# One visit to TensorE's quarters for two pairs of heads, tails and k^T v in rotating banks, and the mean as two products

## The chip, the cores and the metric

The kernel runs on one core of one Trainium2 chip. The metric is device microseconds (us) of one execution. The median of three runs before the change is 900.35 us (900.15 to 900.92).

## The reference

The first part is a linear attention over 8 sequences, 8 heads, 576 rows and 64 columns per head; its result, read as 4608 rows of 512, goes through a gated MLP with 2048 hidden columns. All is float32.

```python
kv = np.einsum('bhsd,bhse->bhde', k, v)
out = np.einsum('bhsd,bhde->bhse', q, kv)
rms = np.sqrt(np.mean(out * out, axis=-1, keepdims=True) + 1e-06)
x = out / rms * g_norm            # then (B,H,S,D) -> (B*S, H*D)
h = x @ w_in
sp = np.maximum(h, 0.0) + np.log1p(np.exp(-np.abs(h)))
g = h * erf(sp)
return g @ w_out
```

## The kernel before

**Groups, batches, pairs.** The MLP works on nine groups of 512 rows, numbered T = 0 to 8. Groups 0 to 7 are the first 512 rows of a sequence each; group 8 collects the eight tails of 64 rows, kept in `x_last`. Groups 0 and 1 run in a plain stage (the loop at L976); from group 2 on the loop at L1143 runs one batch of four hidden units per step. Batch m is b = m mod 4 of group T = m div 4, so batches 8 to 11 are group 2. While group T runs in the MLP, the attention of group T+1 is computed in its batches, one pair of heads (p = 0 to 3) to a batch; that of group 2 runs in the plain stage's group 1.

**A batch on TensorE.** Each batch has eight "products" (L588): four hidden ones (units i = 0 to 3 of this batch: x times w_in) and four results (j = 0 to 3: gated values of the batch before times w_out). A product splits float32 into three float32r parts: eight matmuls of 512 columns into a bank `n_ps`, then four into a bank `m_ps`. ScalarE copies the hidden `n_ps` out (L1192), VectorE adds `m_ps` (L574); results are added into `e` by VectorE alone (L569 or L1129, and L574).

**Banks.** PSUM has eight banks. Six, two named `h` and four `o0` to `o3`, rotate: `pair_of_banks` (L578) takes the first two of the list and puts them at its end, so a product gets its banks back three products later. The other two form the tile `at` of the attention.

**A pair of heads in the attention (L379, `apart` for groups 3 to 7).** Pairs are also numbered i = 4T + p. Its steps in this order:
- `loads`: the DMA starts for k, v and q of the pair after next go onto a list, `to_fetch`. q comes in eight small transfers (L153), laid out so that VectorE's 32x32 transpose (`turn`, L332) gives q^T.
- `visit` (L404): TensorE is used as four quarters of 64x64. Four products of 256 columns give o = q kv (L411); two of 64 columns give the tail's rows (L419); 18 give k^T v of the next pair (L425), all into `at`. A float32 product is two instructions on TensorE. `kv_products` (L338) alternates between the diagonal quarters and the others, so each pair of heads leaves two half sums. Then ScalarE squares o.
- `halve` (L443): VectorE splits the square into two float32r parts. `keep_tail` (L432): one copy of the tail, then `kv_kept` (L354): two copies and one addition that join the half sums of k^T v into `bd_kv`.
- `turn` of the next pair.
- `mean` (L450): four matmuls of 256 columns with the matrix `mean_w`, into the unused half of `at`; ScalarE then does ln, exp and a square.
- `norm` (L481): three VectorE instructions, of which the first (L483) is the last reader of the mean. `split` makes the three parts of x for the next group.

**Where the steps stand.** The loop calls `pieces(place)` with places 0 to 8: place i+1 follows hidden product i, place 5+j follows result j. The steps stand at places (0, 2, 3, 5, 6, 8): loads at 0, visit with halve and keep_tail at 2, that is between hidden products 1 and 2, turn at 3, mean at 5, norm at 6, split at 8. In a group's last batch they are (0, 2, 3, 4, 5, 5, 6). Groups T+1 = 8 use `attention` with other places, no visit, and a mean of two matmuls of 512 columns.

**DMA.** SP issues nearly all transfers in order. At each of the eight fetch places (after product 0, 1, ... 7) it issues the weights that `FETCH` (L1140) names, then two entries of `to_fetch`. The first results of a group's first batch finish the group before, so each is followed by a store that waits for VectorE. w_out has seven buffers; the fourth load for the next batch is the last weight load of the batch.

Of the kernel before, what the change touches and what calls it, by code (L numbers as in the profile page):

```python
# [39 lines left out]
FP32 = mybir.dt.float32  # L40
FP32R = mybir.dt.float32r
I32 = mybir.dt.int32
U32 = mybir.dt.uint32
AF = mybir.ActivationFunctionType
ALU = mybir.AluOpType
PSUM = bass.MemoryType.PSUM

EPS = 1e-6
# [7 lines left out]
FIRST = 2  # L56
# [12 lines left out]
def kernel(  # L69
# [10 lines left out]
    nc = tc.nc  # L80
    P = 128
    B, H, S, D = q.shape
    DM, DF = moe_w_in.shape[0], moe_w_in.shape[1] // 2
    J = 4
    G = J * P
    R = S - G
    NP = H // 2
# [6 lines left out]
    kvp = ctx.enter_context(tc.tile_pool(name="kvp", bufs=2))  # L94
    attp = ctx.enter_context(tc.tile_pool(name="attp", bufs=1))
# [8 lines left out]
    early = early_room.enter_context(tc.tile_pool(name="early", bufs=2))  # L104
# [6 lines left out]
    def exp_ln_table():  # L111
        nc.scalar.preload_act_table_set("natural_log_exp_and_others")

    def softplus_table():
        nc.scalar.preload_act_table_set("softplus")  # L115
# [11 lines left out]
    def load_pair(i, later=False):  # L127
        T, p = divmod(i, NP)
        if T >= B:
            return  # L130
        pool = early if i in (2, 3) else kvp
        for name, got, src in (("k", k_sb, k), ("v", v_sb, v)):
            side = nc.scalar if (i, name) == (0, "v") else nc.sync
            t = got[T, p] = pool.tile([P, CH, D], FP32, name=f"{name}_sb", tag=name)
            start = partial(
                side.dma_start,
                out=t.rearrange("r c d -> r (c d)"),
                in_=src[T, 2 * p : 2 * p + 2].rearrange("h (r c) d -> (h r) (c d)", c=CH),
            )
            if later:  # L140
                to_fetch.append(start)
            else:
                start()
        if T > 0:
            load_q(i)
            return
        t = pool.tile([P, G if pool is early else S], FP32, name="q_sb", tag="q")
        t = q_sb[T, p] = t[:, 0:G].rearrange("p (j h d) -> p j h d", j=J, h=2)
        nc.sync.dma_start(
            out=t, in_=q[T, 2 * p : 2 * p + 2, 0:G, :].rearrange("h (p j) d -> p j h d", j=J)  # L150
        )

    def load_q(i):  # L153


        T, p = divmod(i, NP)
        t = q_sb[T, p] = kvp.tile([P, S], FP32, name="q_sb", tag="q")
        for n in range(P // SQ):
            h, w = divmod(n, D // SQ)
            to = t[n * SQ : n * SQ + SQ].rearrange("a (j b) -> a j b", b=SQ)  # L160
            for head, js in ((1 - h, slice(0, G // 2 // SQ)), (h, slice(G // 2 // SQ, S // SQ))):
                src = q[T, 2 * p + head, :, w * SQ : w * SQ + SQ]
                to_fetch.append(
                    partial(
                        nc.sync.dma_start,
                        out=to[:, js],
                        in_=src.rearrange("(j a) b -> a j b", a=SQ)[:, js],
                    )
                )
# [153 lines left out]
    def halves_of(t):  # L323
        return t.rearrange("p (a t) -> p a t", a=2)

    def kv_of(T, p):
        return bd_kv[:, (T * NP + p) % 2, :]

    def qt_tile(name):
        return attp.tile([P, S], FP32, name=name, tag="qT")  # L330

    def turn(T, p):  # L332

        if T < B:
            qT = ready[T, p] = qt_tile("qT")
            nc.vector.transpose(out=qT, in_=q_sb.pop((T, p)))

    def kv_products(T, p, at, first=0):  # L338


        ks, vs = (x.pop((T, p)) for x in (k_sb, v_sb))
        for c in range(CH):
            for i, rows in enumerate(rows_of):
                half = (i + c + first) % 2
                yield partial(
                    nc.tensor.matmul,
                    at[rows_of[half], 1 if half == i else 0, kv_cols],
                    lhsT=ks[rows, c],
                    rhs=vs[rows, c],
                    start=(c < 2),  # L350
                    stop=(c >= CH - 2),
                )

    def kv_kept(T, p, at):  # L354


        kv = kv_of(T, p).rearrange("p (a e) -> p a e", a=2)
        other = attp.tile([P, 2, D], FP32, name="kv_other", tag="kv_other")
        for i in range(2):
            nc.vector.tensor_copy(out=other[rows_of[i]], in_=at[rows_of[1 - i], ::-1, kv_cols])  # L360
        nc.vector.tensor_tensor(out=kv, in0=at[:, :, kv_cols], in1=other, op=ALU.add)

    def at_tile():
        return at_pool(1).tile([P, 2, G], FP32, name="at_ps", tag="at")

    def prepare(T, p):

        at = at_tile()
        for product_ in kv_products(T, p, at):
            product_()  # L370
        kept.append(partial(kv_kept, T, p, at))

# [6 lines left out]
    def attention(T, p, in_parts=False):  # L379
# [2 lines left out]

        halves = T > 1 or (T == 1 and p > 0)
        quad = T < B
        apart = FIRST < T < B
        then = divmod(T * NP + p + 1, NP)

        def two(t):
            return halves_of(t) if quad else t
# [6 lines left out]
            return ps_now[0].tile([P, G], FP32, name=name, tag="at")  # L396

        def square_tile(name):

            if apart:  # L400
                return attp.tile([P, G], FP32, name=name, tag="sq_lo")
            return qt_tile(name)[:, 0:G]

        def visit():  # L404


            qT = ready.pop((T, p))
            at = st["at"] = at_tile()
            x = halves_of(qT[:, 0:G])
            for a, i in ((0, 0), (0, 1), (1, 0), (1, 1)):  # L410
                nc.tensor.matmul(  # L411
                    at[rows_of[i if a else 1 - i], a, 0 : 2 * P],
                    lhsT=bd[rows_of[i], a * D : (a + 1) * D],
                    rhs=x[rows_of[i], a],
                    start=True,
                    stop=True,
                )
            for s in rows_of:
                nc.tensor.matmul(  # L419
                    at[s, 1, 2 * P : 2 * P + R], lhsT=bd[s, D : 2 * D], rhs=qT[s, G:S], start=True, stop=True  # L420
                )
            st["o"] = at[:, :, 0 : 2 * P]
            if then[0] < B:
                for product_ in kv_products(*then, at, first=1):
                    product_()  # L425
            if apart:
                st["sq"] = x_new.tile([P, G], FP32, name="sq", tag="x")
            else:
                st["sq"] = qT[:, 0:G]
            nc.scalar.activation(two(st["sq"]), st["o"], AF.Square)  # L430

        def keep_tail():  # L432
            nc.vector.tensor_copy(
                out=x_last[:, p, T * R : T * R + R], in_=st["at"][:, 1, 2 * P : 2 * P + R]
            )
            if then[0] < B:
                kv_kept(*then, st["at"])

        def square():
            st["o"], st["sq"] = x_last[:, p, :], square_tile("sq")  # L440
# [73 lines left out]
            split_lower()  # L514

        def loads():
            load_pair(T * NP + p + 2, later=True)

        after = (split_upper, split_lower) if in_parts else (split,)
        if T == B:  # L520
# [1 line left out]

        first_ = (partial(prepare, T, p),) if (T, p) == (1, 0) else ()
        then_ = partial(turn, *then)
        if apart:
            pieces = ((loads,), (visit, halve, keep_tail), (then_,))
            return (*(partial(chain, *group) for group in pieces), mean, norm, *after)
        pieces = (first_, (visit, loads), (halve, keep_tail) if halves else (keep_tail,))
        return (*(partial(chain, *group) for group in pieces), mean, partial(chain, norm, then_), *after)


    def upper(x, high):

        nc.scalar.activation(high, x, AF.Copy, scale=1.0 + 2.0**-13)  # L534
# [14 lines left out]
    def lower(x, high, low, both):  # L549
        lower_only(x, high, low)  # L550
        both_only(high, low, both)
# [26 lines left out]
    def pair_of_banks(*names, turns=True):  # L578
        pair = tuple(
            pool.tile([P, G], FP32, name=name, tag=tag)  # L580
            for name, (pool, tag) in zip(names, banks[:2])
        )
        if turns:
            banks.extend(banks[:2])
            del banks[:2]
        return pair

    def product(weights, moving, turns=True, cuts=()):  # L588

# [104 lines left out]
    def first_group(p):  # L694
# [3 lines left out]

        def kv():
            st["kv"] = at_tile() if p == 0 else ps_now[0].tile([P, 2, G], FP32, name="kv_ps", tag="at")  # L700
            for product_ in kv_products(0, p, st["kv"]):
                product_()

        def kv_out():
# [438 lines left out]
    for m in range(first_batch, batches + 1):  # L1143
# [1 line left out]
        todo = []  # L1145
        last_ = b == NB - 1 and T + 1 < NG
        if T + 1 < NG:
            todo = list(attention(T + 1, b, in_parts=last_))
            if b == 0:
                side = late_r if T % 2 == FIRST % 2 else late  # L1150
                forms = side.tile([P, 3, KC, G], FP32R, name=f"x_forms{(T + 1) % 2}")
                x_forms[T + 1] = [forms[:, i] for i in range(3)]
# [133 lines left out]
```

## Time and profile before

| | |
|---|---|
| median of three runs | 900.35 us |
| profiled execution | 900.88 us, span of its instructions 899.1 us |
| granted TensorE clock | 0.999 |
| TensorE busy | 891.6 us (99%) |
| VectorE busy | 765.5 us (85%) |
| ScalarE busy | 594.8 us (66%) |
| moved by DMA | 259.89 MB, 289 GB/s |

The span runs from the first to the last instruction; the execution's own time also has 1.8 us around it. Busy shares are means over stages: batches 8 to 26 are the stage of the change, batches 27 to 31 and group 8 have other work. Matmuls overlap in the trace, so their cost is read from starts. A wait that ends in "issue" has nothing in the profile to blame.

### The profile page before, as it was taken

What the parts mean: (1) busy time and instruction counts of PE and PEld (TensorE: products, weight loads), DVE (VectorE), ACT (ScalarE), POOL (GpSimd) and SP (SyncE); (2) the same over time, 40 slices, a digit from 0 to 9 for tenths busy, and PEclk for the clock granted to TensorE, in tenths of its full rate; (3) what the DMA queues carried; (4) which work ended last, traced back from release to release, by engine and by line L of the source; (5) the groups of instructions that cost most, each with busy time, mean ns of one, the idle gap of its engine ahead of it and who ended that gap; (6) DMA issues with size and microseconds to landing.
All of it is one profiled execution on the core that took longest, in us unless ns stands there. A gap on an engine that the chain in (4) does not pass through costs nothing.

```text
span 899.1 us, 13468 instructions
## 1 busy us (share of the span) xinstructions
PE 891.6 (99%) x4962; PEld 670.6 (75%) x4962; DVE 765.5 (85%) x1105; ACT 594.8 (66%) x789; POOL 4.7 (1%) x14
## 2 busy tenths in 40 slices
PE   8999999999999999999999999999999999999998
PEld 4444456666788888888888888888888888888887
DVE  5899978899799888888888888888888888886667
ACT  5976677777766666666766666666666666665552
POOL 2000000000000000000000000000000000000000
PEclk9999999999999999999999999999999999999999
DMA  9977318899699987998899979998897787778871
GB/s 285 295 221 232 110 73 320 306 340 351 236 383 356 354 299 263 381 310 302 267 362 337 318 258 327 361 305 293 292 348 274 267 320 296 287 286 315 320 264 49
DMA packets 136929, 259.89 MB, mean 289 GB/s; under 512 B 78816, under 2 KB 87264, under 8 KB 136864
## 3 DMA queue, kind: packets, MB, share of 16 engines
q1 hardware_dynamic: 136128, 258.09, 81.3%
q8 instruction: 39, 0.64, 0.3%
q10 hardware_dynamic: 544, 0.82, 0.2%
q14 instruction: 26, 0.21, 0.1%
q0 software_dynamic: 192, 0.13, 0.1%
HBM read 224.40 MB, written 34.60 MB: 288 GB/s over the span
## 4 chain that ended last, share of the span: by engine, by line
PE 97%; ACT 2%; DVE 1%; issue 0%; DVEq 0%; ACTq 0%
PE n_ps L599 50%; PE m_ps L599 25%; PE o_ps L655 9%; PE h_ps L1021 5%; PE at_ps L411 2%; PE at_ps L425 2%; PE n_ps L918 1%; PE at_ps L463 1%; PE at_ps L464 1%; PE warm_ps L802 1%; PE o_ps L918 0%; ACT w_m L260 0%; PE o_ps L722 0%; DVE w_in_sb L281 0%; DVE w_e L276 0%
## 5 line engine op out<-in xcount | busy, mean ns | idle before, releaser
L599 PE MATMUL n_ps<-w_out_parts,g_forms 128*128 128x512 f32 (+1 forms) x936 | 230.7, 389 | 0.0
L599 PE MATMUL n_ps<-x_forms,w_in_parts 128*128 128x512 f32 x896 | 224.2, 392 | 0.0
L599 PEld LDWEIGHTS n_ps<-w_out_parts,g_forms 128*128 128x128 f32 x936 | 173.8, 188 | 35.3
L599 PEld LDWEIGHTS n_ps<-x_forms,w_in_parts 128*128 128x128 f32 x896 | 166.6, 188 | 35.3
L574 DVE TENSOR_TENSOR h<-m_ps,h 128x512 f32<-128x512 f32 x116 | 78.1, 687 | 60.0 <-PE m_ps L599 56.0
L599 PE MATMUL m_ps<-w_out_parts,g_forms 128*128 128x512 f32 x464 | 124.0, 389 | 0.0
L599 PE MATMUL m_ps<-x_forms,w_in_parts 128*128 128x512 f32 x448 | 119.9, 389 | 0.0
L1192 ACT ACTIVATE h<-n_ps 128x512 f32<-128x512 f32 x112 | 66.1, 593 | 74.9 <-PE n_ps L599 74.7
L1197 ACT ACTIVATE s<-h 128x512 f32<-128x512 f32 x112 | 68.3, 629 | 70.1 <-DVE h L574 70.1
L599 PEld LDWEIGHTS m_ps<-w_out_parts,g_forms 128*128 128x128 f32 x464 | 87.1, 188 | 18.5
L599 PEld LDWEIGHTS m_ps<-x_forms,w_in_parts 128*128 128x128 f32 x448 | 84.1, 188 | 17.9
L574 DVE TENSOR_TENSOR e<-m_ps,e 128x512 f32<-128x512 f32 x116 | 80.1, 692 | 15.2 <-PE m_ps L599 5.4
L655 PE MATMUL o_ps<-w_out_sb,h_sb 128*128 128x512 f32 x192 | 86.8, 595 | 0.0
L540 DVE SCALAR_TENSOR_TENSOR g_forms<-g_forms 128x1024 fp32r<-128x1024 f32 x58 | 71.1, 1225 | 2.0
L537 DVE TENSOR_TENSOR g_forms<-h,g_forms 128x1024 fp32r<-128x1024 f32 x58 | 70.5, 1216 | 1.2 <-ACT g_forms L534 1.1
L534 ACT ACTIVATE g_forms<-h 128x1024 fp32r<-128x1024 f32 x58 | 58.4, 1049 | 15.5 <-PE m_ps L599 11.1
L569 DVE SCALAR_TENSOR_TENSOR e<-n_ps,e 128x512 f32<-128x512 f32 (+1 forms) x89 | 60.3, 678 | 6.9 <-PE n_ps L599 6.9
L1246 DVE TENSOR_TENSOR h<-h,s 128x1024 f32<-128x1024 f32 x56 | 65.9, 1217 | 0.0
L655 PEld LDWEIGHTS o_ps<-w_out_sb,h_sb 128*128 128x128 f32 x192 | 35.5, 190 | 38.3 <-issue 36.9
L1021 PE MATMUL h_ps<-xT,w_in_sb 128*128 128x512 f32 x128 | 57.9, 596 | 1.3 <-DVE w_in_sb L281 1.2
L115 ACT ACT_TABLE_LOAD x43 | 55.2, 1283 | 0.8
L1220 ACT ACTIVATE s<-s 128x1024 f32<-128x1024 f32 x50 | 50.6, 1054 | 0.3
(148 smaller groups left out, 1018.7 us busy)
## 6 DMA issues: line engine op xcount, KB each, us to landing
w_out_parts<-w_out SPq DMA_DIRECT2D x116, 768.0 KB, 7.1
w_in_parts<-w_in SPq DMA_DIRECT2D x112, 768.0 KB, 6.9
w_in<-w_new SPq DMA_DIRECT2D x16, 768.0 KB, 4.5
k_sb<-in_k_dram SPq DMA_DIRECT2D x32, 288.0 KB, 5.9
v_sb<-in_v_dram SPq DMA_DIRECT2D x31, 288.0 KB, 5.7
w_raw<-in_moe_w_in_dram SPq DMA_DIRECT2D x16, 512.0 KB, 5.7
w_raw<-in_moe_w_out_dram SPq DMA_DIRECT2D x8, 1024.0 KB, 4.8
out_dram<-e SPq DMA_DIRECT2D x32, 256.0 KB, 3.7
```

What stands on the lines that cost most here:

```text
L115: nc.scalar.preload_act_table_set("softplus")
L534: nc.scalar.activation(high, x, AF.Copy, scale=1.0 + 2.0**-13)
L537: nc.vector.tensor_tensor(out=low, in0=x, in1=high.bitcast(FP32), op=ALU.subtract)
L540: nc.vector.scalar_tensor_tensor(out=both, in0=low.bitcast(FP32), scalar=SHIFT, in1=high.bitcast(FP32), op0=ALU.mult, op1=ALU.add,)
L569: nc.vector.scalar_tensor_tensor(out=out_, in0=ps, scalar=scale, in1=out_, op0=ALU.mult, op1=ALU.add)
L574: nc.vector.tensor_tensor(out=out_, in0=ps, in1=out_, op=ALU.add)
L599: nc.tensor.matmul(ps[:, cols], lhsT=weights(form, k), rhs=moving(form, k)[:, cols], start=(form == forms[0] and k == 0), stop=(form == fo ...
L655: nc.tensor.matmul(o_ps[j], lhsT=g[:, j * P : j * P + P], rhs=one(w_out_sb, f), start=(f == 0), stop=last,)
L1021: nc.tensor.matmul(plain[i], lhsT=blocks_of(one(w_in_sb, i % FC))[:, c], rhs=xT[T][:, c, :], start=(c == 0), stop=(c == KC - 1),)
L1192: nc.scalar.activation(h[:, i], n_ps, AF.Copy, scale=SHIFT - 1.0)
L1197: nc.scalar.activation(s[:, i], h[:, i], AF.Softplus)
L1246: nc.vector.tensor_tensor(out=part(h, half), in0=part(h, half), in1=part(s, half), op=ALU.mult)
```

## The change

For groups 3 to 7 a function `paired` replaces `attention`. It takes the pairs of heads two by two; "first batch" and "second batch" below mean the batches with even and odd p.

- First batch: at place 0 the sixteen q transfers of the next two pairs go onto the list (for pair 12, the first of group 3, also the transpose of pair 13). At place 2 one visit for both pairs: eight products of 256 columns, which fill `at`, then four tail products and 36 for k^T v of the next two pairs. The tails and k^T v go to two banks from the rotation, diagonal quarters to one, the others to the second, issued two and two. Then the square and halves of the first pair, one copy for both tails, four copies and two additions for both k^T v (`two_kept`), and the k, v transfers of two later pairs. Nothing at place 3.
- Second batch: nothing at place 0; at place 2 the square of the second pair from the same `at`, and its halves; at place 3 two transposes.
- Both: the mean is two matmuls of 512 columns into one bank of the rotation (`next_bank`); norm and split as before, o read from `at`.
- The last visit in `attention` (group 2, pair 3) also makes k^T v of the second pair of group 3. k and v of pairs 13 to 15 are loaded earlier. q^T has two buffers (2304 bytes a partition more), `kv_other` is 512 bytes larger.

```diff
     def qt_tile(name):
-        return attp.tile([P, S], FP32, name=name, tag="qT")
+        return attp.tile([P, S], FP32, name=name, tag="qT", bufs=2)
...
-    def kv_products(T, p, at, first=0):
+    def kv_products(T, p, diagonal, beside, first=0):
...
-                yield partial(
+                yield half == i, partial(
                     nc.tensor.matmul,
-                    at[rows_of[half], 1 if half == i else 0, kv_cols],
+                    (diagonal if half == i else beside)[rows_of[half]],
...
+    def two_kept(diagonal, beside):
+        kv = bd_kv.rearrange("p n (a e) -> p n a e", a=2)
+        other = other_tile(2)
+        for i in range(2):
+            for a, ps in enumerate((diagonal, beside)):
+                nc.vector.tensor_copy(out=other[rows_of[i], :, a], in_=ps[rows_of[1 - i]])
+        for a, ps in enumerate((beside, diagonal)):
+            nc.vector.tensor_tensor(out=kv[:, :, a], in0=ps, in1=other[:, :, a], op=ALU.add)
...
+            if both:
+                for _, product_ in kv_products(then[0], 1, at[:, 1, more_cols], at[:, 0, more_cols]):
+                    product_()
...
         def loads():
-            load_pair(T * NP + p + 2, later=True)
+            i = T * NP + p + 2
+            if i == (FIRST + 1) * NP + 1:
+                load_q(i)
+                load_kv(i + 1)
+                load_kv(i + 2)
+                return
+            load_pair(i, later=True)
+            if i == (FIRST + 1) * NP:
+                load_kv(i + 1)
...
+    def paired(T, p, in_parts=False):
...
+        def visit():
+            at = twice["at"] = at_tile()
+            qs = [ready.pop((T, p + n)) for n in range(2)]
+            for n in range(2):
+                x, bd = halves_of(qs[n][:, 0:G]), kv_of(T, p + n)
+                for a, r in ((0, 0), (0, 1), (1, 0), (1, 1)):
+                    nc.tensor.matmul(
+                        at[rows_of[r if a else 1 - r], a, n * 2 * P : (n + 1) * 2 * P],
...
+            small = pair_of_banks("diag_ps", "off_ps")
...
+            for n in range(2 if more else 0):
+                for on, product_ in kv_products(
+                    *divmod(i + 2 + n, NP), kv_diag(n), kv_off(n), first=1
+                ):
+                    (diag if on else off).append(product_)
+            while diag or off:
+                for some in (diag, off):
+                    for product_ in some[:2]:
+                        product_()
+                    del some[:2]
...
+        def mean(table=True):
+            ms = st["ms"] = next_bank("ms_ps")
+            nc.tensor.matmul(ms, lhsT=mean_w, rhs=st.pop("hi"), start=True, stop=False)
+            nc.tensor.matmul(ms, lhsT=mean_w, rhs=st.pop("lo"), start=False, stop=True)
...
+        def q_loads():
+            if i == (FIRST + 1) * NP:
+                turn(T, 1)
+            for n in range(2):
+                load_q(i + 2 + n)
+
+        def kv_loads():
+            for n in range(2):
+                load_kv(i + 4 + n)
+
+        def turns():
+            for n in range(2):
+                turn(*divmod(i + 1 + n, NP))
+
+        if side == 0:
+            start = (q_loads, partial(chain, visit, square, halve, keep, kv_loads), chain)
+        else:
+            start = (chain, partial(chain, square, halve), turns)
+        return (*start, mean, norm, *after)
...
+    def next_bank(name):
+        pool, tag = banks[0]
+        banks.append(banks.pop(0))
+        return pool.tile([P, G], FP32, name=name, tag=tag)
...
-            todo = list(attention(T + 1, b, in_parts=last_))
+            todo = list((attention if T + 1 == B else paired)(T + 1, b, in_parts=last_))
```

## The prediction

> **What bounds the kernel now.** I read the chain that ended last first: it says which engine's work has to shrink.
>
> ```profile
> PE 97%; ACT 2%; DVE 1%; issue 0%; DVEq 0%; ACTq 0%
> ```
>
> TensorE carries 97% of it, so time is won only by making TensorE's stream shorter, and lost only where it is made to wait. Next I read TensorE's timeline over batch 10 (from 281.60; batches count from group 0, batch 8 starts at 234.13), in the middle of the stage that is changed: start in us, duration of the merged row, operation.
>
> ```profile
> 286.13 1.07 PE L599 MATMUL m_ps<-x_forms,w_in_parts 128*128 128x512 f32 x4
> 287.13 0.66 PE L411 MATMUL at_ps<-qT,bd_kv 64*64 64x256 f32 x8
> 287.61 0.22 PE L425 MATMUL at_ps<-v_sb,k_sb 64*64 64x64 f32 x2
> ...
> 288.30 2.12 PE L599 MATMUL n_ps<-x_forms,w_in_parts 128*128 128x512 f32 x8
> 290.26 1.08 PE L599 MATMUL m_ps<-x_forms,w_in_parts 128*128 128x512 f32 x4
> 291.18 1.98 PE L599 MATMUL n_ps<-x_forms,w_in_parts 128*128 128x512 f32 x8
> ...
> 293.90 1.98 PE L599 MATMUL n_ps<-w_out_parts,g_forms 128*128 128x512 f32 x8
> ...
> 296.62 0.28 PE L463 MATMUL at_ps<-sq_hi,mean_w 128*128 128x256 f32 x1
> ...
> 297.09 2.03 PE L599 MATMUL n_ps<-w_out_parts,g_forms 128*128 128x512 f32 x8
> ...
> 299.87 1.98 PE L599 MATMUL n_ps<-w_out_parts,g_forms 128*128 128x512 f32 x8
> ```
>
> Durations overlap, so I go by starts. An undisturbed product takes 2.72 us (291.18 to 293.90); its last four products, on m_ps, 0.91. The visit costs what lies between 286.13 and 291.18 beyond 0.91 and one product: 5.05 - 3.63 = **1.42**. The mean costs 299.87 - 296.62 - 2.72 = **0.53**. And 8 x 2.72 + 1.42 + 0.53 = 23.71, which is the distance between visits (287.13 to 310.84): TensorE waits for nothing here. The windows give 20.9 us of VectorE and 15.5 of ScalarE in such a batch: both have slack.
>
> **The visit, step by step.** 287.04 (286.13 + 0.91) to 287.13: 0.09 to enter. To 287.61: 0.48 for the eight instructions of q (a float32 product is two), two in each of four quarters. To 288.30: 0.69 for 40 instructions of 64 columns. How much of that is work shows in batch 27, whose visit has only the four tail instructions:
>
> ```profile
> 690.75 0.28 PE L419 MATMUL at_ps<-qT,bd_kv 64*64 64x64 f32 x4
> 690.96 2.12 PE L599 MATMUL n_ps<-x_forms,w_in_parts 128*128 128x512 f32 x8
> ```
>
> There it is 0.21 for two rounds; here 0.69 for ten (40 / 4). So a round takes 0.06 (0.058 by the unrounded starts) and 0.11 is exit. The product after the visit is 0.16 too long. Fixed are 0.09 + 0.11 + 0.16 = 0.36, plus 0.05 of q's first round, whose matmuls are the longest (L411 by tile: 376 to 428 ns).
>
> A visit for two pairs: q 0.48 + 0.43, then 4 tails and 36 k^T v products. With first=1 each pair has ten products for the off-diagonal quarters, eight for the diagonal ones, plus two tails: 20 and 20, issued two and two, so 20 full rounds, 1.16. Sum 0.09 + 0.91 + 1.16 + 0.11 + 0.16 = 2.43 against 2 x 1.42: **0.41 saved, ten times, 4.1 us**. The trace has no visit of this length: from below, nothing of 0.41 is saved if changing pair or bank in mid-visit costs an exit and entry again; from above 0.46, if the rounds also lose the 0.05 at q's second pair. I take 0.41, the row with the same instructions; visits of 4 and 40 small instructions differ by rounds alone.
>
> Two visits change length. That of the third group's last pair (at 215.16, in the plain stage) takes the k^T v of a second pair: 9 or 10 rounds, +0.55. The last one covers batches 26 and 27, which cost 1.42 and 0.95 now: 0.09 + 0.91 + 4 x 0.058 + 0.11 + 0.16 = 1.50, 0.46 better than counted. Net **-0.1**.
>
> **The mean as two products.** The trace has it: in batch 28, for the last group,
>
> ```profile
> 721.57 0.39 PE L463 MATMUL ms_ps<-sq_hi,mean_w 128*128 128x512 f32 x1
> ...
> 724.77 1.98 PE L599 MATMUL n_ps<-w_out_parts,g_forms 128*128 128x512 f32 x8
> ```
>
> 3.20 - 2.72 = 0.48 against 0.53. Saved 0.05, twenty times: **1.0 us**. The Trainium skill, "TensorE: Matmul & The Clock Gate", section "Back-to-back issue gap", speaks against a gain here: 262 cycles for 256 columns and 518 for 512 would make four products 1048 cycles and two 1036, an estimate of 0.005 us a mean and 0.1 in all. The rows of this trace decide for 1.0.
>
> TensorE's sum: 4.1 + 1.0 - 0.1 = **5.0 us**. The second qT tile and the wider kv_other move later tiles in SBUF; no row here depends on a tile's place (L574 takes 0.69 on both of its tiles), so that costs nothing.
>
> **The other engines.** VectorE does the same copies for two pairs at once: one tail copy (0.22 for 64 columns), four of 0.29, two additions of 0.29, about 2.0 against 1.1. In the first batch they replace a transpose (0.77) and stand after both halves of the square, ahead of the third addition to h. Counted from the batch's start: the third product starts at 5.44 + 0.09 + 0.91 + 1.16 + 0.11 = 7.71, the square 0.15 later as now (288.45 after 288.30), then 0.6 of square, 1.15 of halves, 2.0 of copies: 11.7. Result 0, which takes the copies' two banks next, starts at 7.71 + 2.88 + 2.72 = 13.3, and VectorE was idle for 1.34 us before the fourth addition to h, which takes up the delay. The second batch has two transposes (1.54), no copies, and lasts 21.76 + 0.48 = 22.24, as batches 28 to 30 do without a stall; VectorE has 20.9 - 1.1 + 0.8 = 20.6 in it. The Trainium skill, "TensorEngine Tiling (Array Packing)", section "PSUM Bottleneck", warns that copying out of PSUM may become the bound once the array is packed; by that rule the second batch would go at VectorE's pace, still 1.6 us below TensorE's, and the sum would stay.
>
> Banks: six rotate in pairs; a visit now takes two of them and each mean one. The visit's pair held result 3 of the batch before, whose additions end 2.6 us into the batch; it is written at 6.4. The third product gets the first one's pair back after two products instead of three: its m_ps part starts at 9.7, and both additions to h that free these banks end at 7.5 (289.13 in batch 10). The tight place is the mean's bank: it is m_ps of result 3, two products later. VectorE frees it here (batch 13; result 3 starts at 373.73, its m_ps part at 375.54):
>
> ```profile
> 371.21 0.69 DVE L574 TENSOR_TENSOR e<-m_ps,e 128x512 f32<-128x512 f32 x1 [0.23 <-PE m_ps L599]
> 371.82 2.35 DVE L1246 TENSOR_TENSOR h<-h,s 128x1024 f32<-128x1024 f32 x2
> 374.09 0.68 DVE L483 SCALAR_TENSOR_TENSOR u<-at_ps,u 128x512 f32<-128x512 f32 x1
> ```
>
> The end, 374.77, leaves 0.77 us (in a group's last batch, where the mean comes earlier, it is result 2's bank, with 2.1). Bounds: nothing lost, or whatever VectorE is later than 0.77. I take nothing for ordinary batches, since VectorE waits for TensorE just ahead (the 0.23).
>
> **Loads.** SP gets 16 q pieces in a first batch, two at each of its eight places, where k, v and eight pieces filled the first five; four k, v go to the second batch's first two places. The k, v of pairs 13 to 15 go out in the plain stage, where DMA is busy 0.68 of the time (216 to 240). In the second batch the results start at 10.88 us, not 12.30, and need the last w_out. Where stores go out (first batch of a group) SP holds it back until VectorE has finished result 2:
>
> ```profile
> 353.99 0.34 SPq L670 DMA_DIRECT2D out_dram<-e  x1
> 354.38 0.93 SPq L844 DMA_DIRECT2D w_out_parts<-w_out  x2
> ```
>
> The second of these (354.90) landed 6.8 us later, 8.96 into its batch: 1.9 us remain of 3.3. Behind it come the last two q pieces, then the store; k, issued there now, took 7.2 and landed at 10.3, and the second transpose would start at 10.2. In batch 9 the same load was issued at 260.59 and took 9.0: 11.70 into the batch. There results wait up to 0.8; q, landing about 12.5, holds VectorE two more, which pass through the fourth addition, softplus, erf and rms to the mean's bank. The batch before it is 1.0 longer, which gives DMA that much. I charge **0.8 us** once (bounds 0 and 2.5), and nothing for the four others (bounds 0 and 1 each).
>
> **Forecast.** The profiled execution took 900.88 (span 899.1); 5.0 - 0.8 = 4.2 off makes 896.7. It lay 0.53 above the median of the runs, so the median goes from 900.35 to **896.1**.
>
> **Rivals.**
> *Clean:* no load is late: 900.35 - 5.0 = 895.3. For it: waits of TensorE for DMA are absent from the waits. Against: batch 9.
> *The visit saves nothing:* a drain inside the visit at each change of pair or bank. Only the mean remains: 900.35 - 1.0 + 0.1 + 0.8, about 900.2; half saved, 898.2. Against it: within a visit rows follow at 0.06 through all changes of operand.
> *Partly late:* loads cost 0.7 in each of the other four second batches after a store: 896.1 + 2.8 = 898.9.
> *Slower:* the same place, further. The last w_out and q of the second batches after stores (five of them) land late because 16 q pieces of 32 to 40 KB queue where DMA idled. Price: each us beyond 1.9 of added delay is one us of TensorE per batch. To end 0.2% above it must eat 5.0 + 1.8 over five batches, 1.4 each, that is landing 3.3 us later than now, at about 12.2. Batch 9's 11.70 says such landings occur; that DMA is busy only 0.74 of batch 12's second half (341.0 to 352.74), 3.0 us free, speaks against. At 4 us later: 900.35 - 5.0 + 5 x 2.1 = 905.9.
>
> **Chances.** Forecast 0.52, clean 0.16, partly late 0.10, visit saves nothing or half 0.09, slower 0.13. The range from 895.1 (0.2 under clean) to 899.2 holds the first three and part of the fourth, 0.8. 0.2% (1.8 us) is about what a measurement here tells from no change. Faster by more: 0.52 + 0.16 + 0.03 of the halves + 0.08 of partly late = 0.79; the same 0.08; slower 0.13.
>
> **What would show it.** Right: in TensorE's timeline one visit every second batch, about 2.4 us over the products around it; batch pairs of about 24.67 and 22.24; two 512-column products per mean at 0.48; no row of waits of TensorE beyond batch 9. Wrong: the rounds of a long visit over 0.06; a gap ahead of the m_ps part of result 3 (mean's bank), or ahead of result 0 in second batches with w_out or q landing past 10.9. The least certain number is the 0.8.

## The result and the profile after

The changed kernel takes 896.53 us (median of six runs, 895.78 to 896.99), the kernel before beside it 900.61 (six runs). The ratio is 0.9954, its 95% interval 0.9941 to 0.9967. The profiled execution took 896.7, its span 894.9 against 899.1, so the span became 4.2 us shorter. The forecast was 4.2 us less, and 896.1 for the median.

The total agrees better than its terms do. I read the views in the order of the prediction. First the chain that ended last:

```profile
PE 91%; DMA 4%; DVE 3%; ACT 2%; issue 1%; SPq 0%; DVEq 0%; ACTq 0%
```

TensorE carried 97% of it and now carries 91: other engines end waits of TensorE where none did. The six points are not lost time: from each short wait the chain is followed back through whatever ended it, and one load of w_out alone puts 10.7 us on it. Where these waits are comes last. Next the stage of the change, TensorE's timeline in batch 10, which starts at 282.69 (start, duration of the merged row, operation):

```profile
287.22 1.07 PE L773 MATMUL m_ps<-x_forms,w_in_parts 128*128 128x512 f32 x4
288.22 1.09 PE L579 MATMUL at_ps<-qT,bd_kv 64*64 64x256 f32 x16
289.13 0.22 PE L610 MATMUL off_ps<-v_sb,k_sb 64*64 64x64 f32 x2
...
290.25 0.23 PE L610 MATMUL diag_ps<-v_sb,k_sb 64*64 64x64 f32 x2
290.41 2.11 PE L773 MATMUL n_ps<-x_forms,w_in_parts 128*128 128x512 f32 x8
...
293.26 1.98 PE L773 MATMUL n_ps<-x_forms,w_in_parts 128*128 128x512 f32 x8
...
298.70 0.39 PE L645 MATMUL ms_ps<-sq_hi,mean_w 128*128 128x512 f32 x1
298.93 0.39 PE L646 MATMUL ms_ps<-sq_lo,mean_w 128*128 128x512 f32 x1
299.16 2.00 PE L773 MATMUL n_ps<-w_out_parts,g_forms 128*128 128x512 f32 x8
```

The visit now costs 293.26 - 287.22 - 0.91 - 2.72 = 2.41 us once per pair of batches, where it cost 1.42 twice. Its parts are those of the prediction: 0.09 to enter (288.13 to 288.22), 0.91 for q, 1.12 from the first to the last of the small rows (289.13 to 290.25), so 0.059 a round over 19 steps (0.058 forecast), 0.16 from the last of them to the next product, and 0.13 by which that product is too long. The mean goes from 298.70 to 299.16, 0.46, and 0.02 more in the product behind it: 0.48. First batches last 24.65 us and second ones 22.24, in all pairs from batch 9 on, forecast 24.67 and 22.24; each lasted 23.71. The last two batches of the stage went from 23.71 + 23.25 to 23.72 + 22.24.

The tight place of the banks, in batch 13, VectorE and then TensorE:

```profile
374.11 0.68 DVE L658 SCALAR_TENSOR_TENSOR u<-ms_ps,u 128x512 f32<-128x512 f32 x1
```
```profile
375.57 1.07 PE L773 MATMUL m_ps<-w_out_parts,g_forms 128*128 128x512 f32 x4
```

VectorE leaves the mean at 374.79, 0.78 us ahead of the m_ps part (0.77 in the prediction). In the same stretch the last w_out before the second batch was issued at 356.42 and landed 6.8 us later, 8.95 into batch 13 (8.96 before the change). In batches 13, 17, 21 and 25 it landed at 8.5 to 9.4 (8.5 to 9.0 before), ahead of the 10.88 at which the results start.

What is lost lies between 215 and 251 us, in TensorE's waits of the window 220 to 260 (weight loads and matmuls; total, times, longest):

```profile
PEld o_ps L1093 <- DVE g_held L709: 1.0, 2, 0.6
PEld n_ps L773 <- DMA w_out_parts<-w_out: 0.7, 1, 0.7
```

The first is new and was in no forecast. After the mean of group 2's last pair the held products follow: the results of the plain stage's last four hidden units, whose gated values are kept in `g_held`. They are the last work before batch 8, called the held stage here. Before they came at once behind the mean's last matmul; TensorE's timeline before the change:

```profile
222.34 0.28 PE L464 MATMUL at_ps<-sq_lo,mean_w 128*128 128x256 f32 x1
222.46 2.22 PE L918 MATMUL o_ps<-w_place,g_held 128*128 128x512 f32 x8
```

Now, in TensorE's timeline and VectorE's ahead of it:

```profile
222.65 0.28 PE L487 MATMUL at_ps<-sq_lo,mean_w 128*128 128x256 f32 x1
223.16 2.52 PE L1093 MATMUL o_ps<-w_place,g_held 128*128 128x512 f32 x8 [0.22 <-DVE g_held L709]
```
```profile
219.66 0.59 DVE L369 COPY kv_other<-at_ps 64x128 f32<-64x128 f32 x2
220.28 0.29 DVE L370 TENSOR_TENSOR bd_kv<-at_ps,kv_other 128x128 f32<-128x128 f32 x1
220.49 0.68 DVE L743 TENSOR_TENSOR h<-m_ps,h 128x512 f32<-128x512 f32 x1
```

Two copies and an addition (0.88) join the second pair's k^T v ahead of the addition to h and of the parts of g_held that TensorE reads next. With the start of the visit laid on that of the kernel before (215.16 there, 214.90 here), the mean comes 0.57 later, which is the longer visit; the held stage starts another 0.39 later, and is 0.70 behind by its end. (The expectations below were written with a first reading of 0.52 and 0.69.) (The 1.0 of the wait view is that of weight loads, which run beside matmuls, so not all of it is lost.) The second wait is in batch 8, TensorE's timeline:

```profile
248.48 1.52 PE L773 MATMUL n_ps<-w_out_parts,g_forms 128*128 128x512 f32 x6
250.29 0.73 PE L773 MATMUL n_ps<-w_out_parts,g_forms 128*128 128x512 f32 x2 [0.29 <-DMA w_out_parts<-w_out]
```

Result 0's n_ps part takes 2.38 us instead of 1.81: its fourth weights, issued at 239.56, landed at 250.24, after 10.7 us (8.7 before). The wait is 0.57, in batch 8 and not in batch 9, where the forecast had its charge; batch 9 lasts 22.24.

The balance: 9 pairs of batches by 0.53 and the last by 1.00, **5.8 saved**; group 2's visit 0.57 longer, the held stage 0.70, batch 8 0.57, **1.8 lost**: 3.9. The other 0.27 lies in the first 7.5 us of the run, in its first loads, which also differ between kernels that have the same start (by 0.6 between this one and `q_dense` below).

### The profile page after: what moved, and what is told of

It reads as the page before. It is cut to its first block, busy times and chain, and to the rows that moved or that the text cites. A ratio compares the mean times of both kernels' runs of the same rounds, so it can differ in the third digit from the quotient of the medians.

```text
span 894.9 us, 13333 instructions
## 1 busy us (share of the span) xinstructions
PE 886.7 (99%) x4922; PEld 668.5 (75%) x4922; DVE 761.0 (85%) x1095; ACT 594.9 (66%) x789; POOL 4.7 (1%) x14
## 4 chain that ended last, share of the span: by engine, by line
PE 91%; DMA 4%; DVE 3%; ACT 2%; issue 1%; SPq 0%; DVEq 0%; ACTq 0%
PE n_ps L773 48%; PE m_ps L773 24%; PE o_ps L829 8%; PE h_ps L1196 5%; DMA w_in_parts<-w_in 1%; DMA w_out_parts<-w_out 1%; PE at_ps L579 1%; PE off_ps L610 1%; DMA w_in<-w_new 1%; PE warm_ps L977 1%; PE ms_ps L646 1%; PE ms_ps L645 1%; PE at_ps L432 0%; PE at_ps L446 0%; DMA w_out<-w_place 0%
## 5 line engine op out<-in xcount | busy, mean ns | idle before, releaser
L703 ACT ACTIVATE g_forms<-h 128x1024 fp32r<-128x1024 f32 x58 | 58.4, 1049 | 15.5 <-PE m_ps L773 11.1
```

## The experiments

Each diff is against the changed kernel, except where another is named; `...` marks what is left out. Line numbers in rows of an experiment are its own.

Theory: TensorE's sum is right (a visit's fixed cost 0.43, a mean 0.05), and VectorE's three instructions and batch 8's loads lost what is missing. Rivals: the gain comes from elsewhere than the fixed cost of a visit; the held stage is late from the longer visit or DMA.

**One long visit or two short ones** (`two_visits`). The first pair's visit stays at place 2, the second's goes to place 3, one product later; all else stays.

```diff
...
-            start = (q_loads, partial(chain, visit, square, halve, keep, kv_loads), chain)
+            first, second = partial(visit, 0), partial(visit, 1)
+            start = (q_loads, partial(chain, first, square, halve), partial(chain, second, keep, kv_loads))
```

> The changed kernel with its long visit cut in two: the first pair's products stay at place 2, the second pair's go one hidden product later, same products, same banks, same copies. Theory (a visit has a fixed cost of entering and leaving the quarters, 0.36 us, and 0.05 for the first load): first batches go from 24.65 to 25.06, the kernel loses ten times 0.41, about 900.6 us against 896.5. Rival (the gain comes from the separate banks and the order two and two, not from the number of visits): 24.65 and 896.5 stay.

Measured 900.51 us, ratio to before 0.9998 (0.9989 to 1.0008). First batches last 25.08, second ones 22.24. 25.08 - 24.65 = 0.43 is the price of entering and leaving the quarters once more, with the same matmuls. Ten times that is 4.3, and without it next to nothing is left of the gain: the mean's 1.0 goes against the plain stage (batch 8 lasts 25.12 and waits for nothing here). The rival falls. The Trainium skill, "TensorEngine Tiling (Array Packing)", section "Key Properties", says that a change of the tiling mode, and not of the tile alone, drains TensorE. It gives no price. In the rows of batch 10 above, entering and leaving show as 0.09 ahead, 0.10 behind and 0.13 in the next product, and going from pair to pair inside the visit shows nothing: the sixteen instructions of q take 0.91, where two short visits have 0.48 each.

**The mean in four products** (`four_means`), in the changed kernel and in its one bank:

```diff
-            nc.tensor.matmul(ms, lhsT=mean_w, rhs=st.pop("hi"), start=True, stop=False)
-            nc.tensor.matmul(ms, lhsT=mean_w, rhs=st.pop("lo"), start=False, stop=True)
+            hi, lo = (halves_of(st.pop(name)) for name in ("hi", "lo"))
+            for a in range(2):
+                nc.tensor.matmul(halves_of(ms)[:, a], lhsT=mean_w, rhs=hi[:, a], start=True, stop=False)
+                nc.tensor.matmul(halves_of(ms)[:, a], lhsT=mean_w, rhs=lo[:, a], start=False, stop=True)
```

> The changed kernel with the mean again as four products of 256 columns, in the one bank of the rotation. Theory (rows of before): a mean costs 0.53 instead of 0.48, batches 24.70 and 22.29, twenty times 0.05, about 897.6 us. Rival (the cycles that the skill's page gives, 4 x 262 against 2 x 518): 0.005 a mean, 896.6 us.

Measured 897.59 us, ratio to before 0.9968 (0.9956 to 0.998), batches of 24.71 and 22.29. So 0.05 a mean comes from the length of the products, and nothing from the bank. The Trainium skill, "TensorE: Matmul & The Clock Gate", section "Back-to-back issue gap", has isolated gaps of 262 and 518 cycles; by an estimate from these, four products would cost 12 cycles more than two. The batches here say 0.05 us. (The intervals of the two kernels' ratios overlap; the batches decide.)

**The mean alone** (`mean_only`): the kernel before with `next_bank` and the two-product mean for groups 3 to 7.

```diff
...
-            if quad:
+            if apart:
+                ms = next_bank("ms_ps")
+                nc.tensor.matmul(ms, lhsT=mean_w, rhs=st.pop("hi"), start=True, stop=False)
+                nc.tensor.matmul(ms, lhsT=mean_w, rhs=st.pop("lo"), start=False, stop=True)
+                ms = halves_of(ms)
+            elif quad:
...
```

> The kernel before, with one part of the change: the mean of groups 3 to 7 as two products of 512 columns into a bank of the rotation. Theory: batches of 23.66 instead of 23.71 and no new wait, twenty times 0.05, about 899.6 us against 900.6. Rival (the bank that the mean takes comes back too late): a gap ahead of the m_ps part of result 3, batches over 23.71 and a time over 900.6.

Measured 899.58 us, ratio 0.9990 (0.9980 to 0.9999), batches of 23.66, no new wait. The mean is worth the same with and without the longer visit.

**The margin of the mean's bank** (`norm_late`): norm one place later.

```diff
-        places = (0, 2, 3, 5, 6, 8)
+        places = (0, 2, 3, 5, 6 if T + 1 == B else 7, 8)
```

> The changed kernel with norm at place 7 instead of 6, behind VectorE's two additions of result 2, in all but the last batches of groups. It tests the margin of 0.77 us that the mean's bank has. Theory: the bank comes free at about 21.95 in a second batch (as norm did in batches 28 to 30, which have it at place 7), result 3's m_ps part would start at 21.33, so TensorE waits 0.6 to 0.7 in 15 batches: about 10 us more, 906.5. Rival (nothing waits for that bank): 896.5.

Measured 900.83 us, ratio 1.0004 (0.9995 to 1.0013): 4.3 above the changed kernel, where 10 were expected. TensorE waits in second batches only (a group's last batch kept its places). Batch 13, VectorE and TensorE:

```profile
377.32 0.68 DVE L658 SCALAR_TENSOR_TENSOR u<-ms_ps,u 128x512 f32<-128x512 f32 x1
```
```profile
378.05 1.20 PE L773 MATMUL m_ps<-w_out_parts,g_forms 128*128 128x512 f32 x4 [0.51 <-DVE u L658]
```

Batches 13, 17, 21 and 25 last 23.04 instead of 22.24, batch 9 23.49. In the first batch after it VectorE still reads the mean while result 3's m_ps part begins:

```profile
402.78 0.68 DVE L658 SCALAR_TENSOR_TENSOR u<-ms_ps,u 128x512 f32<-128x512 f32 x1
```
```profile
402.84 1.07 PE L773 MATMUL m_ps<-w_out_parts,g_forms 128*128 128x512 f32 x4
```

They overlap without a wait, so these are two banks. The prediction's step "it is m_ps of result 3, two products later" is seen in second batches and not in first ones. In first batches the mean takes one of the two banks named `h`, and the trace does not tell which of the two a product gets.

**VectorE's three instructions left out** (`no_second_copies`): the half sums of the second pair are not joined.

```diff
-            if both:
-                kv_kept(then[0], 1, st["at"], more_cols)
```

> The changed kernel without joining the half sums of k^T v of the second pair of group 3 (two copies and an addition on VectorE are left out; that pair's result is computed from old values). Theory: all of the 0.69 us goes, the visit's own 0.52 stays. Rival (another reason): 0.69 stays.

One run, 895.97 us, span 894.2. The held products start right behind the mean, the held stage has its 0.70 back and the visit's 0.57 stays. The three instructions are the cause.

**The copies on ScalarE** (`copies_on_act`), otherwise the changed kernel:

```diff
...
-                kv_kept(then[0], 1, st["at"], more_cols)
+                kv_kept(then[0], 1, st["at"], more_cols, copy=nc.scalar.copy)
```

> The changed kernel, with the two copies of the second pair's half sums after group 2's last visit done by ScalarE instead of VectorE (the addition stays). Theory (these 0.88 us of VectorE come ahead of the addition to h and the parts g_held, for which TensorE waits in the next stage): 0.59 of them go, and of the 0.69 us that this stage is longer beyond the visit about 0.5 goes; about 896.0 us. Rival (the stage is longer for another reason, such as the k, v loads there): 0.69 stays, 896.5.

Measured 897.51 us, ratio to before 0.9966 (0.9952 to 0.9979): 1.0 slower than the changed kernel instead of 0.5 faster. ScalarE's timeline and then TensorE's:

```profile
220.04 0.53 ACT L369 COPY kv_other<-at_ps 64x128 f32<-64x128 f32 x2 [1.25 <-DVE bd_kv L370]
220.59 0.60 ACT L1211 ACTIVATE h<-n_ps 128x512 f32<-128x512 f32 x1
```
```profile
221.24 0.50 PE L773 MATMUL n_ps<-x_high,w_new 128*128 128x512 f32 x1 [1.19 <-ACT h L1211]
```

The copies waited 1.25 us for VectorE's addition, and queued behind them stood the copy of a hidden product (218.78 in the changed kernel), whose bank TensorE needs next. The old wait shrank, and a new one of 1.19 took its place.

**The copies behind that, and the addition behind h** (`kept_later`). ScalarE makes the two copies after its copy of the hidden product, and VectorE joins them after its addition to h. Both pairs use one `kv_other` tile.

```diff
...
                 nc.scalar.activation(h, n_ps, AF.Copy, scale=SHIFT - 1.0)
+                while after_copy:
+                    after_copy.pop()()
                 add(h, m_ps)
+                while after_add:
+                    after_add.pop()()
```

> The changed kernel, but in the visit of group 2's last pair the two copies of the second pair's k^T v stand on ScalarE behind its copy of the next hidden product, where ScalarE is idle for 1.83 us (219.38 to 221.21 in the changed kernel's profile), and the addition that joins them stands on VectorE behind the next addition to h instead of ahead of it. Theory (the 0.69 us lost in the held stage is VectorE's 0.88 us ahead of the h addition and the parts of g_held): VectorE loses only the 0.29 of the one addition, so the held products wait 0.69 - 0.59 = 0.1 us and the execution is about 0.6 shorter than the changed kernel, 895.9 against 896.5, with no new wait for the h bank, since the copy of the hidden product now comes first. Rival (what lengthens the held stage is the DMA or the longer visit, not VectorE's order): the held products still start 0.69 late and the time stays 896.5.

TensorE's and VectorE's timelines:

```profile
222.62 0.28 PE L503 MATMUL at_ps<-sq_lo,mean_w 128*128 128x256 f32 x1
222.75 2.41 PE L1109 MATMUL o_ps<-w_place,g_held 128*128 128x512 f32 x8
```
```profile
219.76 0.69 DVE L759 TENSOR_TENSOR h<-m_ps,h 128x512 f32<-128x512 f32 x1 [0.15 <-PE m_ps L789]
220.37 0.28 DVE L379 TENSOR_TENSOR bd_kv<-at_ps,kv_other 128x128 f32<-128x128 f32 x1
```

The held products follow the mean at once and the stage ends 0.51 earlier than in the changed kernel, so 0.19 of the 0.70 is left. The span is 894.4, the median 896.14 (five runs), ratio to before 0.9954 (0.994 to 0.9968). The time alone does not tell it from the changed kernel; the trace does.

**The q transfers of batch 8.** Three runs move them. `q_after_visit` lists them behind the visit, so that they go out from place 2 on:

```diff
+            if i > (FIRST + 1) * NP:
+                q_starts()
+
+        def q_starts():
             for n in range(2):
                 load_q(i + 2 + n)
 ...
         def kv_loads():
+            if i == (FIRST + 1) * NP:
+                q_starts()
```

> The changed kernel with the sixteen q transfers of batch 8 put on the list after the visit instead of ahead of batch 8, so that none is issued behind the four w_out loads before place 2. Rival theory (the q pieces in front of or between the loads make the fourth w_out late): the wait of 0.33 to 0.57 us ahead of result 0 in batch 8 goes. My theory (one of the sixteen DMA engines is held by a 16 KB instruction transfer at 245.8 while all are busy, so the load lands when that engine is through): the wait stays between 0.3 and 0.6, and a packet of the instruction queue lies between 239 and 249.

One run, 899.12 us, span 897.3. Batch 8's wait is gone, though the packet of instructions lies where it lay (10.7 us into the batch). So "my theory" failed, by which the packet makes the wait whatever q does, and the rival held for batch 8. But batch 9 lasts 25.45: TensorE waits 0.75 in result 2's n_ps part and 2.21 ahead of result 3's m_ps part.

`fetch_moved` runs 54 more of the small products that warm TensorE up, and lets everything else alone:

```diff
+    for _ in range(54):
+        fill(16)
```

> The changed kernel with 54 small warm-up products of 16 columns more at its start (some 216 instructions more on TensorE; the whole run is some us longer for them, so only batch 8 is read). They move the places in the program at which TensorE's next 16 KB of instructions are fetched by about 40 instructions later, to the end of batch 8's hidden products. Theory (the instruction transfer delays the fourth w_out): no packet of 16 KB while the four loads run, the fourth lands 8.7 to 9.2 us after its issue as before the change, no wait ahead of result 0. Rival: landing at 10.7 and a wait of 0.3 to 0.6 stay.

One run of 922.19 us, of which only batches 8 and 9 are read. Batch 8's wait fell to 0.19, and batch 9 lasted 23.35. The packet of instructions did not leave the four w_out loads as expected: it moved from 10.8 to 11.9 us into batch 8, behind the landing of the third load and still ahead of that of the fourth. The third landed 7.2 us after its issue, as before the change (8.9 in the changed kernel), the fourth still took 10.3. So this run tests the packet on the third load only; the last section has a run in which it falls behind the fourth.

`q_dense` has the q behind the visit too, at three transfers to a place in batch 8, so that they are again all issued within it:

```diff
...
-            fetch_some(2)
+            fetch_some(3 if m == first_batch else 2)
```

> The changed kernel, but in batch 8 the sixteen q transfers are listed after the visit and go out three to a fetch place instead of two, so that they are all issued in batch 8 as before, only later in it. Theory (part of the 0.57 us ahead of result 0's fourth weights in batch 8 comes from the q pieces issued behind that load, and batch 9's 2.9 us in the run with q after the visit from pieces issued as late as batch 9): batch 8 loses at most 0.2, batch 9 stays at 22.24 to 22.5, and the execution is 0.2 to 0.6 shorter than the changed kernel, 895.9 to 896.3. Rival (the late q of batch 9 is set by the traffic and not by the issue): batch 9 grows by over 1 us and the execution is 897.5 or more.

Median 896.14 us, ratio to before 0.9951 (0.9938 to 0.9963), span 893.8 (0.6 of it from the first loads of the run). Batch 8 waits for nothing, batch 9 lasts 22.37.

**Both edits** (`both_later`): `kept_later` and `q_dense` together.

> Both edits together: the second pair's k^T v joined behind the addition to h, and batch 8's q transfers after the visit at three a place. If each holds and they are independent, 0.6 and 0.2 to 0.6 add up: 895.3 to 895.7 against 896.5 of the changed kernel. If the held stage's 0.69 was cover for the loads that follow (batch 8 starts 0.6 earlier while the w_out loads come no earlier), the wait in batch 8 comes back by as much and the time is 895.9 to 896.3.

Median 896.47 us, ratio to before 0.9956 (0.9944 to 0.9969), span 894.7. The held stage has 0.49 of its 0.70 back, batch 8 waits for nothing, and batch 9 lasts 23.13: the two gains do not add up, and what is lost is lost in batch 9, which neither account expected. VectorE's timeline in batch 9 (from 259.27) and TensorE's:

```profile
271.90 0.78 DVE L345 STREAM_TRANSPOSE qT<-q_sb 128x576 f32<-128x576 f32 x1 [2.54 <-DMA v_sb<-in_v_dram]
...
280.62 0.68 DVE L674 SCALAR_TENSOR_TENSOR u<-ms_ps,u 128x512 f32<-128x512 f32 x1
```
```profile
281.35 1.21 PE L795 MATMUL m_ps<-w_out_parts,g_forms 128*128 128x512 f32 x4 [0.59 <-DVE u L674]
```

The last q piece landed at 271.78, 12.51 us into the batch, the second transpose starts behind it, and all that VectorE does after it arrives late at the mean's bank. (The row blames v; its transfers land at 273.2 and later, q's at 271.78, and in every run below this transpose starts within 0.15 of q's landing.) So the time that was won ahead of these loads is given back in them. With the runs above this makes a row: landing of the last q piece, in us from the start of batch 9, and what the batch lost over 22.24.

| run | last q lands at | lost |
|---|---|---|
| `two_visits` | 11.10 | 0.00 |
| changed kernel | 11.41 | 0.00 |
| `copies_on_act` | 11.57 | 0.03 |
| `no_second_copies` | 11.62 | 0.02 |
| `q_dense` | 11.76 | 0.13 |
| `kept_later` | 11.82 | 0.19 |
| `both_later` | 12.51 | 0.89 |
| `fetch_moved` | 12.74 | 1.11 |
| `q_after_visit` | 14.94 | 3.21 |

Up to about 11.6 it costs next to nothing, and from there each us costs about one. No version measured here beats the changed kernel by more than a measurement can tell.

## Why the prediction was right, and where its steps were not

- **The visit.** Right. 0.41 saved each, by rounds of 0.058 and a fixed cost of 0.41; measured 0.42, and `two_visits` gives the fixed cost by itself as 0.43. The trace of before already had two visits of different length, and their difference priced a third length.
- **The mean.** Right: 0.05 each; the single edits `four_means` and `mean_only` moved the batches by 0.05 both ways, as forecast; the times went by 1.1 us (896.53 to 897.59) and 0.9 (ratio 0.9990), neither of them well clear of noise. The other estimate that the prediction gave, 0.1 in all, was wrong here.
- **Group 2's visit.** Its length was right (+0.55, measured 0.57). The step that failed is what was left out of it: the same edit puts a second `kv_kept` on VectorE, and "**The other engines**" reckoned VectorE for batches of the main stage only. In the plain stage the addition to h and g_held stand behind it, and TensorE needs g_held right after the mean. This is the missed term, 0.70 us.
- **Banks.** Nothing was lost, as forecast, with 0.78 us to spare where 0.77 was forecast. The argument was stricter than need be: `norm_late` shows that bank as the limit in second batches, and not in first ones.
- **Loads.** The charge was 0.8, measured 0.57, but in another place. It said that w_out and q are late in batch 9, with w_out 11.70 into it and q at "about 12.5". There w_out landed at 10.87, just as the results start, and q at 11.41, and nothing was lost; the fourth w_out in batch 8 came late instead, which the step did not look at, since it took batch 8 for the batch that gives DMA time. That the size was near is luck. The mechanism of the step is real: `both_later` has q at 12.51, and loses 0.89 through the fourth addition, softplus and erf to the mean's bank, nearly the charge of 0.8.
- **The four other second batches** lost nothing, as forecast; *partly late* and *slower* had been kept for them, and w_out landed there at 8.5 to 9.4.
- **The sum.** 5.56 were forecast for the stage and 5.8 came; 0.70 was missed; the loads cost 0.23 less; and 0.27 came from the first loads of the run. These errors have both signs and cancel, so the profiled execution met its 896.7 by luck in part, and the 0.4 between the medians (896.1 and 896.53) says little of the terms. *Clean* fell by the 1.3 of VectorE and loads; *the visit saves nothing* fell with `two_visits`.

Open: why batch 8's fourth w_out takes 10 us and more. The table in the last section has it for all runs. With the sixteen q pieces in place and the packet of instructions behind it the load takes 9.3 (`two_visits`), with the packet ahead of its landing and q listed later 10.0, with both 10.3 to 10.7; before the change 8.7. By these the packet is worth 1.1 to 1.4 and the place of the pieces 0.3 to 0.7. That is read across runs that differ in other things too; none moves the packet alone past this load.

## What to carry to other kernels

Price a change of array shape by two visits of different length that the trace already holds: the difference is work, the rest is fixed, and only the fixed part is saved by merging visits. An edit that lengthens one step at the seam between two stages must be followed there by itself, on every engine whose queue it enters, because the slack of the main loop says nothing of the seam. Time won ahead of a stretch that waits for DMA was given back in it here: find the landing from which each us costs one, as in the table, before moving loads.

## What the runs showed of the hardware

One thing was not expected. In batch 8 a packet of instructions appears among the DMA engines' data. The DMA view of the changed kernel from 245.0 to 246.5 has (packets, MB, share of 16 engines):

```profile
q1 hardware_dynamic: 117, 0.63, 100.5%
q8 instruction: 1, 0.02, 3.8%
```

One packet, 3.8% of 16 engines' 1.5 us: 0.9 us of one engine. In the kernel before there is none of this queue from 238 to 249, where these loads were in flight. In `two_visits` it comes at 248.9, just as the fourth load lands, and the issue of that load reads (KB, us to landing):

```profile
w_out_parts<-w_out SPq DMA_DIRECT2D x1, 768.0 KB, 9.3
```

All runs side by side, in us; the packet's start is counted from the start of batch 8, "took" is from a load's issue to its landing, and the wait is TensorE's in result 0:

| run | q pieces of batch 8 | packet starts | third w_out took | fourth took | wait |
|---|---|---|---|---|---|
| before | eight, not sixteen | 1.9, ahead of these loads | 7.2 | 8.7 | 0 |
| `two_visits` | ahead of the visit | 13.7 | 7.2 | 9.3 | 0 |
| `q_dense` | after it | 10.9 | 7.1 | 10.0 | 0.01 |
| `q_after_visit`, `both_later` | after it | 10.7 | 8.8 | 10.0 | 0 |
| `fetch_moved` | ahead | 11.9 | 7.2 | 10.3 | 0.19 |
| changed kernel, `four_means`, `norm_late`, `no_second_copies`, `copies_on_act`, `kept_later` | ahead | 10.6 to 10.8 | 8.7 to 8.9 | 10.4 to 10.7 | 0.33 to 0.57 |

Undisturbed, the third load lands 11.1 us into the batch. It is late where the packet starts 0.3 us or more ahead of that, and on time where the packet starts under 0.2 ahead or later. The fourth takes 10 us or more wherever the packet starts clearly ahead of its landing. That the packet delays these loads is the reading that fits all rows; for the third load `fetch_moved` comes near to showing it by itself, for the fourth no run does.
